# S and dP as rows: streaming transposed K and V past a 32-column weight in a decode attention backward

## The chip, the cores and the metric

One core of one Trainium2 chip runs the whole kernel. The metric is the device time of one execution in microseconds. The profile is one profiled execution of the same program; times inside it count from the start of its span.

## The reference

One token (B = Sq = 1, D = 640) goes through attention over a cache of 4096 keys in 32 heads of 128, and through a dense layer with Mish (F = 1728); a sigmoid gate mixes both. Computed are the output and the gradients of x, both caches, all weights, the bias and the gate. In bf16, K and V are 32 MB each, and dK and dV are as large.

```
q = (x @ wq) per head;  S = q . K * 128**-0.5;  p = softmax(S);  o = p @ V;  a = o @ wo
h = x @ w1 + b1;  b = mish(h) @ w2;  g = sigmoid(x . gate_w);  out = g*a + (1-g)*b
backward, per head, with do = (g*dy) @ wo.T:
  dP = do . V;  D = sum(p*dP);  dS = p*(dP - D)
  dV = p (outer) do;  dK = dS (outer) q*scale;  dq = dS @ K * scale
  dwo = o (outer) g*dy;  dwq = x (outer) dq;  dx, dw1, db1, dw2, dgate_w
```

## The kernel before

A head's K and V lie in SBUF as 128 partitions with 32 rows of 128 each (`Kn`, `Vn`; `KBUFS` = 4 and `VBUFS` = 3 buffers). The order of the work is written out by hand: a loop over heads, in groups of four (G = 4, NG = 8), and an epilogue for the last head. Each engine runs its instructions in that order, and nearly all transfers are issued by SP (SyncE) in that order too.

For each head:

- `k_tr` and `v_tr` (by `tr_block`, L511) transpose K and V. Pairs of bf16 are taken as one f32 word, four 128x128 words go through TensorE into one of two `tr` banks, and ScalarE copies them (L517) to `KT` or `VT`, which share one buffer. A head's K is four such blocks.
- `scores` and `dP` (by `cols_mm`, L519) make S and dP as 128x32 columns: 32 matmuls each, with a 128x128 piece of the transposed tile as the weights and a window of `qz` or `doz` (q or do, zero-padded) as the 32 columns that stream. `scores` also takes the row maximum on VectorE.
- `softmax` (L548) takes the maximum over partitions by a transpose, `exps` the exponentials on ScalarE, `dP` the products with dP on VectorE (`pj`), `zd_mm` the two sums over partitions, `probs` (L571) makes p and dS on VectorE.
- `dv_out` and `dk_out` write a head's dV and dK as two VectorE products each (L583) into `o_sb` (four buffers) and store it (L593).
- `dq_o` (L605) multiplies K with dS and V with p: 16 matmuls of 128x512 whose weights are 4 columns wide and go to column groups 0, 32, 64 and 96 of one PSUM bank. `od_cp` copies the bank, `dqo_mm` transposes the copy in the next head, `dqo_red` adds it up.

In the loop over h, V of head h is transposed at the head's start, and K of head h+1 after `dP(h)`. A head ends with `load_k(h + 4)` and `load_v(h + 3)`. Steps of the group (`g_*` for the next group's q and do, `f_*` for the last group's weight gradients) and of the dense layer (`mlp_some` with a budget of VectorE time, `dw2_some`) are placed by the head's number hh in its group. wq comes in three pieces of 2, 4 and 2 groups (`WQP`), in buffers of their own size; the gradient of each is written in place and stored from there.

A transfer waits for the one that used its semaphore before it; transfers from SP and ACT share eight such semaphores in turn.

Of the kernel before, what the change touches and what calls it, by code (L numbers as in the profile page):

```python
# [7 lines left out]
ACT = mybir.ActivationFunctionType  # L8
# [8 lines left out]
def kernel(  # L17
# [25 lines left out]
    P = 128  # L43
# [19 lines left out]
    JH = J // 2  # L63
    W = 32

# [24 lines left out]
    const = ctx.enter_context(tc.tile_pool(name="const", bufs=1))  # L90
    KBUFS, VBUFS = 4, 3
    kv_in = ctx.enter_context(tc.tile_pool(name="kv_in", bufs=KBUFS))
# [23 lines left out]

    WQP = [(0, 2), (2, 6), (6, NG)]
    assert NG == 8
# [110 lines left out]
    def pair_mm(col):  # L229
        ps = grp([P, 2, G], F32, "pair_ps")  # L230
        for par in range(2):
            nc.tensor.matmul(ps[:, par, :], lhsT=unzip[:, par, :], rhs=col[:], start=True, stop=True)
        return ps

    def pair_cp(z, ps):
        for par in range(2):
            nc.vector.tensor_tensor(z[:, :, J - 2 + par * J:J + par * J],  # L237
                                    ps[:, par, :].unsqueeze(2).to_broadcast([P, G, 2]),
                                    half[:].unsqueeze(1).to_broadcast([P, G, 2]), ALU.mult)
# [7 lines left out]
    def g_qpair_cp(g):  # L247
        pair_cp(qz, groups[g].pop("pair"))

# [3 lines left out]
    def g_dopair(g):  # L253
        pair_cp(doz, pair_mm(groups[g].pop("col")))

# [252 lines left out]

    S_ps, DP_ps, OD_ps = {}, {}, {}
    KT, VT, dgms, es, zds, p4s, ds4s = {}, {}, {}, {}, {}, {}, {}  # L510
# [7 lines left out]

    def cols_mm(out, T, z):  # L519
        Tb = T[:].rearrange("p c r -> p (c r)").bitcast(BF16).rearrange("p (c r a) -> p c r a", r=P, a=2)  # L520
        for c in range(J // 2):
            for par in range(2):
                a = J - 2 - 2 * c + par * J
                nc.tensor.matmul(out, lhsT=Tb[:, c, :, par], rhs=z[:, a:a + J],  # L524
                                 start=(c == 0 and par == 0), stop=(c == J // 2 - 1 and par == 1))

    def k_tr(h, c):
        if h < H:
            if c == 0:
                KT[h] = kvT.tile([P, J // 2, P], F32, name="KT", tag="T")  # L530
            tr_block(kts[h], KT[h], c)

# [4 lines left out]

    def scores(h):
        if h >= H:
            return  # L540
        S_ps[h] = s_ps.tile([P, J], F32, name="S", tag="S")
        cols_mm(S_ps[h][:], KT.pop(h), qz[:, h % G, :])
        m32 = small.tile([P, 1], F32, name="m32", tag="m32")
        nc.vector.reduce_max(m32[:], S_ps[h][:], axis=AX.X)
        dgms[h] = small.tile([P, 1], F32, name="m_s", tag="m_s")
        nc.vector.tensor_scalar(dgms[h][:], m32[:], scale, None, ALU.mult)
# [8 lines left out]
    def exps(h, negM):  # L555
        es[h] = small.tile([P, J], BF16, name="e_bf", tag="e_bf")
        zds[h] = small.tile([P, 2], F32, name="zd", tag="zd")
        nc.scalar.activation(es[h][:], S_ps.pop(h)[:], ACT.Exp, bias=negM[:], scale=scale, accum_out=zds[h][:, 0:1])

    def dP(h):  # L560
        DP_ps[h] = s_ps.tile([P, J], F32, name="DP", tag="DP")
        cols_mm(DP_ps[h][:], VT.pop(h), doz[:, h % G, :])
        pj = small.tile([P, J], F32, name="pj", tag="pj")
        nc.vector.scalar_tensor_tensor(pj[:], in0=DP_ps[h][:], scalar=1.0, in1=es[h][:],  # L564
                                       op0=ALU.mult, op1=ALU.mult, accum_out=zds[h][:, 1:2])
# [4 lines left out]
    def probs(h, mx):  # L570
        rz = small.tile([P, 1], F32, name="rz", tag="rz")  # L571
        nc.vector.reciprocal(rz[:], mx[:, P:P + 1])
        negD = small.tile([P, 1], F32, name="negD", tag="negD")
        nc.vector.tensor_scalar(negD[:], mx[:, P + 1:P + 2], rz[:], -1.0, ALU.mult, ALU.mult)
        p4s[h] = p4b[h % 3][:, 0:J * 4].rearrange("p (j t) -> p j t", t=4)
        nc.vector.tensor_scalar(p4s[h], es.pop(h)[:].unsqueeze(2).to_broadcast([P, J, 4]), rz[:], None, ALU.mult)
        ds4s[h] = ds4b[h % 3][:, 0:J * 4].rearrange("p (j t) -> p j t", t=4)
        nc.vector.scalar_tensor_tensor(ds4s[h], in0=DP_ps.pop(h)[:].unsqueeze(2).to_broadcast([P, J, 4]),
                                       scalar=negD[:], in1=p4s[h], op0=ALU.add, op1=ALU.mult)
        zds.pop(h)  # L580
# [35 lines left out]
    def od_cp(h):  # L616
        od_sb[h] = small.tile([P, 4, Dh], F32, name="row_sb", tag="row_sb", bufs=1)
        nc.scalar.copy(od_sb[h][:].rearrange("p j d -> p (j d)"), od4[:])  # L618
# [85 lines left out]
    for hh in range(G):  # L704
        g_do(0, hh)
    scores(0)
    g_dodiag(0)
    g_dobc(0)
    g_docol(0)
    g_dopair(0)  # L710
    g_qs(0)

    for h in range(H - 1):
        g, hh = h // G, h % G
        nx, pv = g + 1 < NG, g > 0
        v_tr(h, 0)
        if hh == 0 and pv:
            g_docol(g)
        if hh == 3 and nx:
            g_qcol(g + 1)  # L720
        if h > 0:
            dqo_mm(h - 1)
        v_tr(h, 1)
        mx, negM = softmax(h)
        if h > 0:
            dqo_red(h - 1)
        if hh == 0 and pv:
            g_dopair(g)
        if h > 0:
            dk_out(h - 1)  # L730
        v_tr(h, 2)
        v_tr(h, 3)
        exps(h, negM)
        dP(h)
        k_tr(h + 1, 0)
        k_tr(h + 1, 1)
        zd_mm(h, mx)
# [94 lines left out]
    l_dqbf(0, 3)  # L832
    v_tr(h, 2)
    v_tr(h, 3)
    exps(h, negM)
    dP(h)
    zd_mm(h, mx)
    f_bc(g, 0, 3)
# [83 lines left out]
```

## Time and profile before

| | |
|---|---|
| runs | 406.1, 406.25, 406.46 us; median 406.25 |
| profiled execution, span | 403.4 us, 10458 instructions (the page has no other time for it) |
| busy: PE, PEld, DVE, ACT | 306.3, 242.3, 312.1, 224.0 us |
| HBM read and written | 82.03 and 82.03 MB, 407 GB/s over the span |
| DMA packets | 27380, 164.72 MB |
| chain that ended last | DMA 60%, PE 15%, DVE 14%, ACT 4%, issue 3% |

PE is TensorE's matmuls and PEld its weight loads; DVE is VectorE, ACT ScalarE. A row of a group shows line, engine and operation, out<-in, count | busy us, mean ns of one | idle time just before them and what ended it. A row of waits is: us in total, times, longest. A row of stretches is: length, then the busy us (and count) of PE, PEld, DVE, ACT and POOL, the granted TensorE clock, the DMA share and GB/s. The 40 slices of the page are 10.1 us each.

### The profile page before, as it was taken

What the parts mean: (1) busy time and instruction counts of PE and PEld (TensorE: products, weight loads), DVE (VectorE), ACT (ScalarE), POOL (GpSimd) and SP (SyncE); (2) the same over time, 40 slices, a digit from 0 to 9 for tenths busy, and PEclk for the clock granted to TensorE, in tenths of its full rate; (3) what the DMA queues carried; (4) which work ended last, traced back from release to release, by engine and by line L of the source; (5) the groups of instructions that cost most, each with busy time, mean ns of one, the idle gap of its engine ahead of it and who ended that gap; (6) DMA issues with size and microseconds to landing.
All of it is one profiled execution on the core that took longest, in us unless ns stands there. A gap on an engine that the chain in (4) does not pass through costs nothing.

```text
span 403.4 us, 10458 instructions
## 1 busy us (share of the span) xinstructions
PE 306.3 (76%) x4278; PEld 242.3 (60%) x4285; DVE 312.1 (77%) x875; ACT 224.0 (56%) x447; POOL 9.9 (2%) x25
## 2 busy tenths in 40 slices
PE   2689999859888996869787788778798794889500
PEld 1477677647677875656675566656686474677300
DVE  3636877958988797998998888669999984996730
ACT  2256566645555564655577574877676363475600
POOL 3000001000000000000000011000000000000000
PEclk9999999998989899998999997989989898699855
DMA  8999999999999999999999999999999999999892
GB/s 296 425 415 423 424 423 412 416 423 423 418 427 425 422 415 426 424 424 425 425 423 424 425 421 425 416 427 424 424 423 425 423 423 425 420 409 417 365 399 86
DMA packets 27380, 164.72 MB, mean 408 GB/s; under 512 B 2884, under 2 KB 3013, under 8 KB 10950
## 3 DMA queue, kind: packets, MB, share of 16 engines
q1 hardware_dynamic: 27026, 164.05, 97.9%
q8 instruction: 33, 0.54, 0.5%
q14 instruction: 13, 0.11, 0.1%
q0 software_dynamic: 256, 0.01, 0.0%
q10 hardware_dynamic: 52, 0.01, 0.0%
HBM read 82.03 MB, written 82.03 MB: 407 GB/s over the span
## 4 chain that ended last, share of the span: by engine, by line
DMA 60%; PE 15%; DVE 14%; ACT 4%; issue 3%; DVEq 0%; SPq 0%; ACTq 0%
DMA out_dram<-o_sb 38%; DMA Vn<-in_A_v_cache_dram 15%; DVE o_sb L583 8%; PE tr L516 6%; DMA wo_g<-in_A_wo_dram 5%; DMA wq_p<-in_A_wq_dram 2%; DVE junk L259 2%; PE od L611 2%; ACT VT L517 2%; PE dqo_ps L624 1%; ACT KT L517 1%; PE q_ps L212 1%; PE S L524 1%; PE h_ps L409 1%; DVE wq_p L379 1%
## 5 line engine op out<-in xcount | busy, mean ns | idle before, releaser
L517 ACT COPY KT<-tr 128x512 f32<-128x512 f32 x128 | 69.2, 588 | 54.7 <-PE tr L516 54.7
L516 PE MATMUL tr<-ident_f,Vn 128*128 128x128 f32 x512 | 83.3, 297 | 18.6 <-DMA Vn<-in_A_v_cache_dram 12.2
L517 ACT COPY VT<-tr 128x512 f32<-128x512 f32 x128 | 72.2, 585 | 38.2 <-PE tr L516 37.1
L583 DVE TENSOR_TENSOR o_sb<-qs_row,ds 128x2048 bf16<-128x2048 bf16 x64 | 75.4, 1220 | 18.9 <-DMA out_dram<-o_sb 18.7
L516 PEld LDWEIGHTS tr<-ident_f,Vn 128*128 128x128 f32 x512 | 62.7, 152 | 34.1 <-ACT VT L517 12.2
L516 PE MATMUL tr<-ident_f,Kn 128*128 128x128 f32 x512 | 75.1, 293 | 8.2 <-DMA Kn<-in_A_k_cache_dram 5.7
L583 DVE TENSOR_TENSOR o_sb<-do_row,p 128x2048 bf16<-128x2048 bf16 x64 | 75.3, 1218 | 0.0
L516 PEld LDWEIGHTS tr<-ident_f,Kn 128*128 128x128 f32 x512 | 59.9, 151 | 11.2 <-DVE ident_f L169 5.7
L618 ACT COPY row_sb<-od 128x512 f32<-128x512 f32 x32 | 18.8, 586 | 39.5 <-PE od L611 39.5
L524 PE MATMUL DP<-doz,VT 128*128 128x32 bf16 x1024 | 36.2, 178 | 2.8
L524 PEld LDWEIGHTS <-KT 128*128 128x128 bf16 x1024 | 33.4, 98 | 6.5 <-ACT KT L517 3.3
L524 PE MATMUL S<-qz,KT 128*128 128x32 bf16 x1024 | 35.6, 179 | 1.9 <-DVE qz L237 0.2
L524 PEld LDWEIGHTS <-VT 128*128 128x128 bf16 x1024 | 32.9, 97 | 6.4 <-ACT VT L517 5.7
L611 PE MATMUL od<-Kn,ds 128*4 128x512 bf16 x256 | 36.1, 407 | 0.0
L611 PE MATMUL od<-Vn,p 128*4 128x512 bf16 x256 | 36.1, 407 | 0.0
L552 DVE TENSOR_REDUCE negM<-mx 128x1 f32<-128x128 f32 x32 | 9.3, 289 | 23.9 <-PE mx L550 22.0
L259 DVE SCALAR_TENSOR_TENSOR junk<-wo_g,da_bc 128x640 bf16<-128x640 bf16 x32 | 26.3, 821 | 0.4
L568 PE MATMUL mx<-zd,ones_f 128*128 128x2 f32 x64 | 11.1, 243 | 18.9 <-DVE pj L564 18.8
L387 ACT ACTIVATE wo_g<-da_bc,o 128x640 bf16<-128x640 bf16 x32 | 24.6, 822 | 0.0
L329 DVE SCALAR_TENSOR_TENSOR junk<-wq_p,dq_bc 128x512 bf16<-128x512 bf16 x35 | 24.1, 687 | 0.5
L624 PE MATMUL dqo_ps<-ident_f,row_sb 128*128 128x128 f32 x128 | 21.7, 295 | 3.1 <-ACT dh_bc L493 1.1
L568 PEld LDWEIGHTS mx<-zd,ones_f 128*128 128x128 f32 x64 | 9.9, 196 | 22.3 <-DVE pj L564 22.0
(169 smaller groups left out, 326.1 us busy)
## 6 DMA issues: line engine op xcount, KB each, us to landing
out_dram<-o_sb SPq DMA_DIRECT2D x64, 1024.0 KB, 18.6
Kn<-in_A_k_cache_dram SPq DMA_DIRECT2D x32, 1024.0 KB, 19.2
Vn<-in_A_v_cache_dram SPq DMA_DIRECT2D x32, 1024.0 KB, 19.3
wo_g<-in_A_wo_dram SPq DMA_DIRECT2D x8, 640.0 KB, 19.7
out_dram<-wo_g SPq DMA_DIRECT2D x8, 640.0 KB, 19.2
wq_p<-in_A_wq_dram SPq DMA_DIRECT2D x2, 1280.0 KB, 8.4
wq_p<-in_A_wq_dram SPq DMA_DIRECT2D x1, 2560.0 KB
out_dram<-wq_p SPq DMA_DIRECT2D x2, 1280.0 KB
```

The costliest lines, as they stand in the source:

```text
L259: nc.vector.scalar_tensor_tensor(junk[:], in0=wos[g][:, hh, :], scalar=1.0, in1=da_bc[:], op0=ALU.mult, op1=ALU.mult, accum_out=gp["do_col ...
L329: nc.vector.scalar_tensor_tensor(junk[:, cs], in0=wqs[g][:, c, cs], scalar=1.0, in1=gp["dq_bc"][:, cs], op0=ALU.mult, op1=ALU.mult, accum_ ...
L387: nc.scalar.activation(wos[g][:, hh, :], da_bc[:], ACT.Copy, scale=groups[g]["o4"][:, hh:hh + 1])
L516: nc.tensor.transpose(tp[:, t, :], words[:, t * P:(t + 1) * P], ident_f[:])
L517: nc.scalar.copy(dst[:, c * (TB // 2):(c + 1) * (TB // 2), :], tp[:])
L524: nc.tensor.matmul(out, lhsT=Tb[:, c, :, par], rhs=z[:, a:a + J], start=(c == 0 and par == 0), stop=(c == J // 2 - 1 and par == 1))
L552: nc.vector.tensor_reduce(negM[:], mx[:, 0:P], axis=AX.X, op=ALU.max, negate=True)
L568: nc.tensor.matmul(mx[:, P:P + 2], lhsT=ones_f[:], rhs=zds[h][:], start=True, stop=True)
L583: nc.vector.tensor_tensor(dst[:, a:b, :].rearrange("p j (k t) -> p j k t", t=4), row.rearrange("p (k t) -> p k t", t=4).unsqueeze(1).to_br ...
L611: nc.tensor.matmul(od4[32 * c:32 * c + 4, :], lhsT=c4[:, 4 * jb:4 * jb + 16].rearrange("p (j t) -> p t j", t=4)[:, 0, :], rhs=N[:, jb:jb + ...
L618: nc.scalar.copy(od_sb[h][:].rearrange("p j d -> p (j d)"), od4[:])
L624: nc.tensor.transpose(od_sb[h][:, j * (P - 1):j * (P - 1) + P], t[:, j, :], ident_f[:])
```

## The change

S and dP become rows. q and do each are put into a weight of 128x32 per parity of the bf16 pair (`qz` and `doz`, zeros elsewhere), so that one such matmul streams 512 columns of `KT` (four words c, 4+c, 8+c, 12+c of the 16) and gives S in some of its 32 output rows. Four column groups c and two parities are eight matmuls for S, and eight more for dP accumulate into other rows of the same PSUM bank `rw`. `rows_cp` copies the bank on ScalarE, `rows_tr` transposes it back in four pieces to `sd`, whose strided columns are S and dP. The maximum of S moves behind it (`maxes`), and the product with dP stands alone (`pjs`).

V of head h+1 is transposed in head h, after K of h+1, and the first head's V in the prologue. V gets a fourth buffer and `load_v(h + 4)`. wq comes in four pieces of two groups in two buffers. Group steps change places: do of the next group is made ready earlier. The last 64 rows of dw2 leave in four transfers from ACT's queue.

```
-    KBUFS, VBUFS = 4, 3
+    KBUFS, VBUFS = 4, 4
-    WQP = [(0, 2), (2, 6), (6, NG)]
+    WQP = [(g, g + 2) for g in range(0, NG, 2)]
-        wqp[k] = wts.tile([P, RC, (z - a) * GD], BF16, name="wq_p", tag=f"wq_{z - a}", bufs=1)
+        wqp[k] = wts.tile([P, RC, (z - a) * GD], BF16, name="wq_p", tag="wq_p", bufs=2)
     load_k(3)
+    load_v(3)
-    qz = const.tile([P, G, 3 * J - 2], BF16, name="qz")
-    doz = const.tile([P, G, 3 * J - 2], BF16, name="doz")
+    qz = const.tile([P, G, 2, 2, 16], BF16, name="qz")
+    doz = const.tile([P, G, 2, 2, 16], BF16, name="doz")
-    def pair_cp(z, ps):
+    def pair_cp(z, ps, at):
-            nc.vector.tensor_tensor(z[:, :, J - 2 + par * J:J + par * J],
+            nc.vector.tensor_tensor(z[:, :, par, :, at],
...
-    def cols_mm(out, T, z):
-        Tb = T[:].rearrange("p c r -> p (c r)").bitcast(BF16).rearrange("p (c r a) -> p c r a", r=P, a=2)
-        for c in range(J // 2):
-            for par in range(2):
-                a = J - 2 - 2 * c + par * J
-                nc.tensor.matmul(out, lhsT=Tb[:, c, :, par], rhs=z[:, a:a + J],
-                                 start=(c == 0 and par == 0), stop=(c == J // 2 - 1 and par == 1))
+    rw = s_ps.tile([P, 4 * P], F32, name="rw", tag="rw")
+    def rows_mm(T, z, first):
+        Tb = T[:].rearrange("p k r -> p (k r)").bitcast(BF16).rearrange("p (t c r a) -> p c a t r", t=4, c=4, a=2)
+        for par in range(2):
+            for c in range(4):
+                nc.tensor.matmul(rw[32 * c:32 * (c + 1), :], lhsT=z[:, par, :, :].rearrange("p m u -> p (m u)"), rhs=Tb[:, c, par, :, :],
+                                 start=first and par == 0, stop=not first and par == 1)
-    def scores(h):
...
+    def k_rows(h):
+        rows_mm(KT.pop(h), qz[:, h % G], True)
+    def v_rows(h):
+        rows_mm(VT.pop(h), doz[:, h % G], False)
+    def rows_cp(h):
+        rw_sb[h] = small.tile([P, 4, P], F32, name="row_sb", tag="row_sb", bufs=2)
+        nc.scalar.copy(rw_sb[h][:].rearrange("p t r -> p (t r)"), rw[:])
+    def rows_tr(h):
+        t = rw_sb.pop(h)
+        x = s_ps.tile([P, 4, P], F32, name="sd", tag="sd")
+        for j in range(4):
+            nc.tensor.transpose(x[:, j, :], t[:, j, :], ident_f[:])
+        v = x[:].rearrange("p t r -> p (t r)").rearrange("p (j u) -> p j u", u=16)
+        sd[h] = (v[:, :, 0], v[:, :, 1])
+    def maxes(h):
+        m32 = small.tile([P, 1], F32, name="m32", tag="m32")
+        nc.vector.tensor_reduce(m32[:], sd[h][0], axis=AX.X, op=ALU.max)
...
```

The loop's body after the change, without the group's steps:

```
        k_tr(h + 1, 0)
        dqo_mm(h - 1)
        k_tr(h + 1, 1)
        mx, negM = softmax(h)
        dqo_red(h - 1)
        dk_out(h - 1)
        k_tr(h + 1, 2)
        k_tr(h + 1, 3)
        exps(h, negM)
        k_rows(h + 1)
        pjs(h)
        v_tr(h + 1, 0)
        v_tr(h + 1, 1)
        zd_mm(h, mx)
        probs(h, mx)
        v_tr(h + 1, 2)
        v_tr(h + 1, 3)
        dv_out(h)
        v_rows(h + 1)
        dq_o(h)
        rows_cp(h + 1)
        rows_tr(h + 1)
        od_cp(h)
        maxes(h + 1)
        load_k(h + KBUFS)
        load_v(h + VBUFS)
```

And of the rest:

```
         if h == H - 4:
...
-            nc.sync.dma_start(out_8[FM:F, :], w2_sb[0:FT, FR, :])
+            for a, b in ((0, 2), (2, 5), (5, 9), (9, FT)):
+                nc.scalar.dma_start(out_8[FM + a:FM + b, :], w2_sb[a:b, FR, :])
...
-            if g in (0, 4):
-                load_wqp(g // 4 + 1)
+            if g % 2 == 0 and g + 4 <= NG:
+                load_wqp(g // 2 + 1)
```

In the epilogue the last head's `v_tr` and `dP` are gone; they lie in the loop.

More of the change, by code (lines that the diff above doesn't have):

```diff
@@ L63 @@
     JH = J // 2
-    W = 32
     Kv = A_k_cache.rearrange("b h (p j) d -> (b h) p j d", p=P)
@@ L115 @@
     wqp = {}
-    WQP = [(0, 2), (2, 6), (6, NG)]
-    assert NG == 8
+    WQP = [(g, g + 2) for g in range(0, NG, 2)]
+    assert NG % 2 == 0
     def load_wqp(k):
         a, z = WQP[k]
-        wqp[k] = wts.tile([P, RC, (z - a) * GD], BF16, name="wq_p", tag=f"wq_{z - a}", bufs=1)
+        wqp[k] = wts.tile([P, RC, (z - a) * GD], BF16, name="wq_p", tag="wq_p", bufs=2)
         for g in range(a, z):
@@ L247, in g_qpair_cp @@
     def g_qpair_cp(g):
-        pair_cp(qz, groups[g].pop("pair"))
+        pair_cp(qz, groups[g].pop("pair"), 0)
     def g_docol(g):
@@ L253, in g_dopair, with g_dopair_cp @@
     def g_dopair(g):
-        pair_cp(doz, pair_mm(groups[g].pop("col")))
+        groups[g]["pair"] = pair_mm(groups[g].pop("col"))
+    def g_dopair_cp(g):
+        pair_cp(doz, groups[g].pop("pair"), 1)
     def g_do(g, hh):
@@ L507, in m_dw2 @@
         nc.scalar.activation(w2_sb[0:n, fc, :], db_bc[0:n, :], ACT.Copy, scale=act_f[0:n, fc:fc + 1])
-    S_ps, DP_ps, OD_ps = {}, {}, {}
     KT, VT, dgms, es, zds, p4s, ds4s = {}, {}, {}, {}, {}, {}, {}
@@ L517, in tr_block @@
         nc.scalar.copy(dst[:, c * (TB // 2):(c + 1) * (TB // 2), :], tp[:])
-    def cols_mm(out, T, z):
-        Tb = T[:].rearrange("p c r -> p (c r)").bitcast(BF16).rearrange("p (c r a) -> p c r a", r=P, a=2)
-        for c in range(J // 2):
-            for par in range(2):
-                a = J - 2 - 2 * c + par * J
-                nc.tensor.matmul(out, lhsT=Tb[:, c, :, par], rhs=z[:, a:a + J],
-                                 start=(c == 0 and par == 0), stop=(c == J // 2 - 1 and par == 1))
+    rw = s_ps.tile([P, 4 * P], F32, name="rw", tag="rw")
+    rw_sb, sd = {}, {}
+    def rows_mm(T, z, first):
[4 more added lines that the diff above has]
+                                 start=first and par == 0, stop=not first and par == 1)
     def k_tr(h, c):
[L528 to L531, printed above, removed]
+        if c == 0:
+            KT[h] = kvT.tile([P, J // 2, P], F32, name="KT", tag="T")
+        tr_block(kts[h], KT[h], c)
     def v_tr(h, c):
@@ L536, in v_tr @@
         tr_block(vts[h], VT[h], c)
-    def scores(h):
[L539 to L542, printed above, removed]
+    def k_rows(h):
[13 more added lines that the diff above has]
+    def maxes(h):
         m32 = small.tile([P, 1], F32, name="m32", tag="m32")
-        nc.vector.reduce_max(m32[:], S_ps[h][:], axis=AX.X)
+        nc.vector.tensor_reduce(m32[:], sd[h][0], axis=AX.X, op=ALU.max)
         dgms[h] = small.tile([P, 1], F32, name="m_s", tag="m_s")
@@ L557, in exps, with pjs @@
         zds[h] = small.tile([P, 2], F32, name="zd", tag="zd")
[L558 to L562, printed above, removed]
+        nc.scalar.activation(es[h][:], sd[h][0], ACT.Exp, bias=negM[:], scale=scale, accum_out=zds[h][:, 0:1])
+    def pjs(h):
         pj = small.tile([P, J], F32, name="pj", tag="pj")
-        nc.vector.scalar_tensor_tensor(pj[:], in0=DP_ps[h][:], scalar=1.0, in1=es[h][:],
+        nc.vector.scalar_tensor_tensor(pj[:], in0=sd[h][1], scalar=1.0, in1=es[h][:],
                                        op0=ALU.mult, op1=ALU.mult, accum_out=zds[h][:, 1:2])
@@ L577, in probs @@
         ds4s[h] = ds4b[h % 3][:, 0:J * 4].rearrange("p (j t) -> p j t", t=4)
-        nc.vector.scalar_tensor_tensor(ds4s[h], in0=DP_ps.pop(h)[:].unsqueeze(2).to_broadcast([P, J, 4]),
+        nc.vector.scalar_tensor_tensor(ds4s[h], in0=sd.pop(h)[1].unsqueeze(2).to_broadcast([P, J, 4]),
                                        scalar=negD[:], in1=p4s[h], op0=ALU.add, op1=ALU.mult)
@@ L616, in od_cp @@
     def od_cp(h):
-        od_sb[h] = small.tile([P, 4, Dh], F32, name="row_sb", tag="row_sb", bufs=1)
+        od_sb[h] = small.tile([P, 4, Dh], F32, name="row_sb", tag="row_sb", bufs=2)
         nc.scalar.copy(od_sb[h][:].rearrange("p j d -> p (j d)"), od4[:])
@@ L705 @@
         g_do(0, hh)
-    scores(0)
+    k_rows(0)
     g_dodiag(0)
@@ L710 @@
     g_dopair(0)
+    g_dopair_cp(0)
+    for c in range(4):
+        v_tr(0, c)
+    v_rows(0)
+    rows_cp(0)
+    rows_tr(0)
+    maxes(0)
     g_qs(0)
@@ L715 @@
         nx, pv = g + 1 < NG, g > 0
-        v_tr(h, 0)
-        if hh == 0 and pv:
-            g_docol(g)
+        k_tr(h + 1, 0)
+        if h > 0:
+            dqo_mm(h - 1)
+        k_tr(h + 1, 1)
         if hh == 3 and nx:
             g_qcol(g + 1)
-        if h > 0:
-            dqo_mm(h - 1)
-        v_tr(h, 1)
         mx, negM = softmax(h)
@@ L726 @@
             dqo_red(h - 1)
-        if hh == 0 and pv:
-            g_dopair(g)
         if h > 0:
             dk_out(h - 1)
-        v_tr(h, 2)
-        v_tr(h, 3)
-        exps(h, negM)
-        dP(h)
-        k_tr(h + 1, 0)
-        k_tr(h + 1, 1)
+        k_tr(h + 1, 2)
+        k_tr(h + 1, 3)
+        if hh == 3 and nx:
+            g_qpair(g + 1)
+            g_qpair_cp(g + 1)
+            g_docol(g + 1)
+        exps(h, negM)
+        k_rows(h + 1)
+        pjs(h)
+        v_tr(h + 1, 0)
+        if hh == 3 and nx:
+            g_dopair(g + 1)
+            g_dopair_cp(g + 1)
+        v_tr(h + 1, 1)
         zd_mm(h, mx)
@@ L742 @@
             f_dx(g - 1, 3)
+        if hh == 1 and nx:
+            g_do(g + 1, 0)
         if hh == 2 and nx:
-            g_do(g + 1, 0)
-        if hh == 3 and nx:
-            g_qpair(g + 1)
             g_do(g + 1, 3)
         probs(h, mx)
-        if hh == 3 and nx:
-            g_qpair_cp(g + 1)
         if hh == 0 and pv:
@@ L753 @@
             f_o4c(g - 1)
-        k_tr(h + 1, 2)
-        k_tr(h + 1, 3)
+        v_tr(h + 1, 2)
+        v_tr(h + 1, 3)
         if hh == 0 and pv:
             f_bc(g - 1)
-        if hh == 3 and nx:
+        if hh == 2 and nx:
             g_dodiag(g + 1)
         dv_out(h)
-        scores(h + 1)
-        if hh == 3 and nx:
+        v_rows(h + 1)
+        if hh == 2 and nx:
             g_dobc(g + 1)
         dq_o(h)
+        rows_cp(h + 1)
+        rows_tr(h + 1)
         od_cp(h)
+        maxes(h + 1)
         load_k(h + KBUFS)
@@ L799 @@
                 f_dwo_st(g - 1)
-            budget = 2.7
-        if hh == 2:
             if nx:
@@ L804 @@
                 g_do(g + 1, 2)
+            budget = 0.9
+        if hh == 2:
+            if nx:
                 g_q(g + 1)
-            budget = 0.9
+            budget = 2.7
         if hh == 3:
-            if g in (0, 4):
-                load_wqp(g // 4 + 1)
+            if g % 2 == 0 and g + 4 <= NG:
+                load_wqp(g // 2 + 1)
             if g + 2 < NG:
@@ L823 @@
     nc.vector.tensor_tensor(gg[:], g_all[:], omg_all[:], ALU.mult)
-    v_tr(h, 0)
+    mx, negM = softmax(h)
     dqo_mm(h - 1)
-    v_tr(h, 1)
-    mx, negM = softmax(h)
+    exps(h, negM)
+    pjs(h)
+    zd_mm(h, mx)
     dqo_red(h - 1)
@@ L832 @@
     l_dqbf(0, 3)
[L833 to L837, printed above, removed]
     f_bc(g, 0, 3)
```

## The prediction

> **What bounds the kernel now.** I read the page first: busy time, the slices, the DMA queues.
>
> ```profile
> PE 306.3 (76%) x4278; PEld 242.3 (60%) x4285; DVE 312.1 (77%) x875; ACT 224.0 (56%) x447; POOL 9.9 (2%) x25
> ...
> DMA  8999999999999999999999999999999999999892
> GB/s 296 425 415 423 424 423 412 416 423 423 418 427 425 422 415 426 424 424 425 425 423 424 425 421 425 416 427 424 424 423 425 423 423 425 420 409 417 365 399 86
> ...
> q8 instruction: 33, 0.54, 0.5%
> ```
>
> No engine is busy above 77%, while the sixteen DMA engines are full from the first slice to the last but two, near 425 GB/s. So bytes set the time: 164.72 MB at 425 GB/s are 388 us, of 403.4. The rest must lie at the ends, so next the busy time by stretches:
>
> ```profile
> 350.00:372.00 22.00, 19.50 (x301) 15.96 (x298) 18.29 (x52) 15.85 (x33) 0.00 (x0) 1.00 1.01 411
> 372.00:378.00 6.00, 4.24 (x66) 2.87 (x65) 3.44 (x9) 2.59 (x7) 0.00 (x0) 1.00 0.81 333
> ...
> 394.00:396.00 2.00, 0.00 (x0) 0.00 (x0) 0.00 (x0) 0.00 (x0) 0.00 (x0) 0.50 0.53 218
> 396.00:398.00 2.00, 0.00 (x0) 0.00 (x0) 0.00 (x0) 0.00 (x0) 0.00 (x0) 0.50 0.07 28
> 398.00:400.00 2.00, 0.00 (x0) 0.00 (x0) 0.00 (x0) 0.00 (x0) 0.00 (x0) 0.50 0.07 29
> 400.00:402.00 2.00, 0.00 (x0) 0.00 (x0) 0.00 (x0) 0.00 (x0) 0.00 (x0) 0.50 0.06 25
> ```
>
> The last two columns are DMA share and GB/s. From 396 to 402 the share is 0.07, one engine of sixteen: fifteen are done at 395.0 to 395.7, one at 402.1. The trace's records of single packets show how that one fell behind. A `wo` transfer has packets of 5120 bytes that nothing else of that time has, so its end can be timed per engine. First and last engine end 9.7 and 10.9; then 103.1 and 105.5; 148.7 and 153.2; 212.2 and 219.0; 279.0 and 288.4; 327.5 and 338.8; 367.6 and 379.3. The late engine loses 11.7 us while the leaders keep the pace of their bytes. Its packets run back to back: it never lacks work, its own load sets the end, and only its load or a hole in its queue can move the time. At 372 to 378 the leaders starve instead, waiting for stores whose last sixteenth is with the late engine; so the gap at the end is 6.4 to 7.1, not 11.7.
>
> Then the waits, for the room that compute has:
>
> ```profile
> DVE o_sb L583 <- DMA out_dram<-o_sb: 18.7, 10, 5.9
> ...
> PE tr L516 <- DMA Vn<-in_A_v_cache_dram: 12.2, 12, 1.8
> ```
>
> Those 30.9 us over some 26 heads are 1.2 us a head. From head 5 to head 27 `dq_o` starts 11.44 us apart (78.8 to 330.4), so compute alone would need about 10.2.
>
> **The change, part by part.** First PE:
>
> ```profile
> L611 PE MATMUL od<-Kn,ds 128*4 128x512 bf16 x256 | 36.1, 407 | 0.0
> L524 PE MATMUL S<-qz,KT 128*128 128x32 bf16 x1024 | 35.6, 179 | 1.9 <-DVE qz L237 0.2
> L524 PEld LDWEIGHTS <-KT 128*128 128x128 bf16 x1024 | 33.4, 98 | 6.5 <-ACT KT L517 3.3
> L624 PE MATMUL dqo_ps<-ident_f,row_sb 128*128 128x128 f32 x128 | 21.7, 295 | 3.1 <-ACT dh_bc L493 1.1
> ```
>
> Gone are 2048 matmuls with a weight load each; new are 32 x 16 = 512 row matmuls and 32 x 4 = 128 transposes, each with its load. PE's 4278 + 4285 = 8563 instructions become 8563 - 4096 + 1280 = 5747.
>
> On PE's path this saves nothing. The old S needed KT block by block: 24 of its 32 matmuls ran under ACT's fourth copy, and `od` began 0.36 us after that copy (37.75 to 38.11). A row matmul of group c reads words c, 4+c, 8+c, 12+c, one from each copy, so all eight wait for the fourth. Their price is not in the trace; the nearest row is `od`, also 512 columns into four column groups, where fours start 0.21 us apart in the timeline (29.56, 29.77, 29.99, 30.20): eight are 2 x 0.21 + 0.17 = 0.6. One after another at `od`'s 0.38 they would be 3.0. I take 0.6, as the groups and width are `od`'s; the stride of two elements in the streamed side is what could make it 1.0. So +0.24 per use, twice a head; `rows_tr` adds 0.5 to 0.66 (L624's four). Together about 1.1 us a head: 10.2 + 1.1 = 11.3, just under 11.44, and so hidden by DMA. ACT gets a copy of 128x512 a head, 32 x 0.586 = 19 us, to 243 of 403; it stands before `od_cp`, and that one's readers come a head later. Behind the waiting row matmuls on PE stand `v_tr` and `zd_mm`; DVE's `probs` waits for those, and the 1.1 has it all in. `maxes` now waits for `rows_tr`, under `dv_out` (2 x 1.22) on DVE; without that cover it is 0.66 more.
>
> PE's instructions are themselves DMA traffic. Queue q8's 33 packets are 16,384 bytes each; 8563 / 33 = 259 instructions a packet, so 5747 make 22. The first comes at 27.5 us, the last at 372.4, 10 to 11 apart, each 0.9 to 1.1 us long (0.5% of sixteen engines' span is 32 us of one engine). The late engine's delays come in lumps of about 0.6 us, near many of these packets, and 0.6 is what 16,384 bytes cost at its pace (8192 in 0.306). Before the first packet the ends lie within 1.1 us. So I charge the lag to the fetches: 11.7 / 33 = 0.355 each, 11 fewer: -3.9. The bounds: spread evenly, 11 x 0.96 / 16 = -0.7; all on the late engine, 11 x 0.96, capped by the others' end at 395.7, -6.4. I take the measured slope.
>
> The Trainium skill, "Runtime: NRT & Kernel Launch", Instruction fetch mechanics, has the same blocks (16 KiB, 256 instructions) and says that crossing one is mostly hidden; by it this term is 0 and the sum 406.65. It speaks of the sequencer's wait, and no run here shows that wait apart.
>
> Smaller parts. `wq` in four pieces: the middle 2.62 MB move in rows of 2048 bytes, which follow each other every 80 ns, instead of 4096 every 155; per engine 80 x 80 for 40 x 155, +0.2 on the load and +0.2 on the store, on the late engine too: +0.4. The 64 rows of `out_8` in four pieces: 0 to 8 rows an engine for 4, at some 0.05 us a row, -0.2 to +0.2: 0. They move from SP to ACT (some 0.3 us each, in one head, where ACT has room), and take four of the eight semaphores that transfers share; SP's store of dK of head 27 may so wait for them, which the seven transfers still in flight cover (17 us); without them it would cost some 7. V and K of head h+4 are issued together and V's fourth buffer replaces the head by which it is now read earlier: 0. `g_do`, `g_dodiag` and the budgets change places between heads: 0, the same work under the same cover.
>
> The start is where a hole could open. Today the first store is issued at 30.7 us, and the loads ahead of it run dry at 36.6 to 38.6 (the ends of `w2`'s 6400-byte packets). The loop's first head now comes after four more transposed blocks and the row chain: two more pairs of blocks of K and V (some 1.4 each), the row copy and transposes (1.3), and the waits: I get 36.5. V of head 3 adds 1.05 MB, 2.5 us, so the loads last to 39 or 41. Some 2 us of room: 0, with a bound of +3.
>
> Sum against the profiled execution: 403.4 - 3.9 + 0.4 = 399.9. The median of the runs, 406.25, lies 2.85 above that span, taken as unchanged: 402.75, say 402.7.
>
> **The rivals.** *The lag is the engine's own.* For: other engines lose time too (at 327 ten are 4 to 6 us behind the first five), more than 33 fetches explain evenly; five packets of this size I could place (at 149.1, 192.9, 235.9, 260.8, 326.7) delayed another engine. Against: no lag before the first fetch, no lump after the last, only 0.5 us from 339 to 379, when PE was slow. Then the change is +0.4 less at most 0.7: 406.0 to 406.7, no difference that a measurement of this kernel can tell (0.2%, 0.8 us). "DMA: Bandwidth & Descriptors" of the Trainium skill, Latency and other measured facts, says that engines 7 and 15 are usually slower, which would be this case. Chance 0.13.
>
> *PE's head becomes longer than DMA's.* The place is `k_rows` and `v_rows`, which stop PE until the fourth copy. Room is 1.2 us a head; from there each further 0.1 us costs 29 x 0.1. Row matmuls of 0.8 instead of 0.6 give 1.5 added, +0.3 a head: +9, less part of the 3.5: 411 to 415. Half speed (1.0) gives about 425. For: the room is nearly spent; a hole at the start would come on top. Against: `od` runs this very shape in fours, DVE (9.75 us a head) is left alone. Chance 0.33, from just over 407 up.
>
> *All fetches sit on the late engine:* 406.25 - 6.4 + 0.4 = 400.2. Against: the five just placed. Chance 0.04.
>
> **How the numbers follow.** The forecast has 0.50, from 401 to 405: its slope is uncertain by a third. It and the last rival are faster, 0.54; the engine's own lag is the same, 0.13; the longer head is slower, 0.33. The likeliest case gives 402.7. Below 400.2 I leave 0.03; above 411 half of the slower case: 0.16.
>
> **What would show it.** Right: q8 near 22 packets, one engine alone at the end for some 3 us instead of 6.4, DMA still near 425 in the middle, row matmuls in fours 0.21 apart. Wrong: 22 packets and the same lone engine for 6 us (the lag is its own); or slices in the middle below 415 GB/s and PE's waits on ACT's copies above the DMA waits (a longer head); or a dip near 36 to 42 us (the start).

## The result, and the profile after

The changed kernel takes 421.51 us (median; 418.22 to 423.30), the kernel before 406.36 on the same chip: 1.0369 times, 95% interval 1.0324 to 1.0415, or some 15 us slower. Forecast were 402.7 us and a range that ended at 411. Of the rivals it was the longer head, and worse than its 411 to 415. Of all runs below, one of ten of e7_early_start, three of six of e8_late_do (its profile too) and one of twelve of e11_fill_copy_wait lie over 1.5% above the fastest of their kernel and are left out of the figures.

The page after, in the parts that were shown of before (busy time; DMA slices of 10.5 us; the fetch queue), and the chain that ended last:

```profile
span 421.5 us, 7650 instructions
PE 307.5 (73%) x2870; PEld 215.2 (51%) x2877; DVE 316.1 (75%) x875; ACT 241.5 (57%) x479; POOL 10.7 (3%) x25
...
DMA  7999997999999999999989999999989999979997
GB/s 276 429 417 421 389 428 307 361 411 415 426 416 421 410 376 427 388 401 417 424 356 362 424 413 426 417 417 424 372 326 333 416 397 417 384 292 422 405 363 286
...
q8 instruction: 22, 0.36, 0.3%
...
PE 43%; DVE 34%; ACT 15%; issue 3%; DMA 2%; DVEq 0%; ACTq 0%; SPq 0%
```

The chain was DMA 60% before and is DMA 2% now. Sixteen slices lie under 400 GB/s, spread over the whole span; before there were four, the first and three at the end. PE and VectorE are busy for hardly longer than before (+1.2 and +4.0 us), and ScalarE for 17.5 us more, the added copies; so what costs time is not more work but more waiting. The waits of after (us in total, times, longest) say for what:

```profile
DVE m L561 <- PE sd L555: 29.0, 24, 6.9
...
PE rw L528 <- ACT VT L519: 20.8, 32, 0.7
...
PE rw L528 <- ACT KT L519: 16.9, 25, 0.7
...
ACT VT L519 <- PE pair_ps L232: 16.6, 7, 3.2
...
PE rw L528 <- DVE qz L237: 10.5, 7, 1.9
...
DVE doz L237 <- PE pair_ps L232: 10.1, 8, 2.0
...
PE tr L518 <- DMA Kn<-in_A_k_cache_dram: 5.9, 1, 5.9
```

The two rows of before that gave the forecast its room, VectorE waiting for stores (18.7) and PE for V (12.2), are gone. PE's one wait for K is the first load. In their place stand waits of engine for engine. The groups of the row matmuls and of the maximum (line, engine, operation, count | busy, mean ns of one | idle time before them and what ended it):

```profile
L528 PE MATMUL rw<-KT,qz 128*32 128x512 bf16 x256 | 22.3, 425 | 27.4 <-ACT KT L519 16.9
L528 PE MATMUL rw<-VT,doz 128*32 128x512 bf16 x256 | 22.8, 434 | 20.8 <-ACT VT L519 20.8
...
L561 DVE TENSOR_REDUCE m<-sd 128x1 f32<-128x32 f32 x32 | 6.1, 190 | 29.7 <-PE sd L555 29.0
```

Two kinds of wait stand out: the row matmuls of nearly every head wait for the fourth copy (20.8 + 16.9 = 37.7 us), and seven or eight times, once a group, `qz`, `doz` and the copies behind them wait for the columns of the next group's q and do (10.5, 10.1 and 16.6 us).

The timeline of one such head, hh = 3, in order (start, us, engine, what; in brackets the idle time before it):

```profile
207.18 0.25 PE L223 MATMUL col_ps<-ones_bf,q_row 1*128 1x1 bf16 x4
...
207.85 0.16 DVE L226 CAST col<-col_ps 128x4 bf16<-128x4 f32 x1
...
208.20 2.35 DVE L598 TENSOR_TENSOR o_sb<-qs_row,ds 128x2048 bf16<-128x2048 bf16 x2
208.42 0.19 PE L232 MATMUL pair_ps<-col,unzip 128*128 128x4 bf16 x2
...
210.47 0.26 DVE L237 TENSOR_TENSOR qz<-pair_ps,half 128x8 bf16<-128x8 f32 x2
...
210.71 0.88 PE L528 MATMUL rw<-KT,qz 128*32 128x512 bf16 x8 [1.92 <-DVE qz L237]
...
212.72 0.27 DVE L237 TENSOR_TENSOR doz<-pair_ps,half 128x8 bf16<-128x8 f32 x2 [1.84 <-PE pair_ps L232]
212.73 0.58 ACT L519 COPY VT<-tr 128x512 f32<-128x512 f32 x1 [3.22 <-PE pair_ps L232]
```

The pairs are ready on PE at 208.6, but their copy into `qz` stands behind `dk_out` on VectorE (208.20 to 210.55), and PE's `k_rows` stands still for it. Then do's columns run PE, VectorE, PE, VectorE once more, with ScalarE's V copies behind them. Before, `qz` was wanted at the end of this head and `doz` only in the next, and do's columns were made there too, at the start of hh = 0.

**Where 18.1 us of span went**, by the starts of `dq_o` in the two profiled executions: head 0 at 29.6 before and 37.4 after, +7.8; from there to head 5, 49.3 and 55.5, +6.2; heads 5 to 28, 269.5 and 280.9, +11.4; to the last head +1.0; and from there to the end 28.1 and 19.9, -8.3, since DMA has less left to drain. From head 5 to 27 the pitch is 12.30 us (270.5 / 22) for 11.44, and in after nothing in that stretch waits for DMA: 12.3 is what compute needs, on the average of these heads.

### The profile page after: what moved, and what is told of

It is laid out like the page before. It is cut to its first block, busy times and chain, and to the rows that moved or that the text cites. A ratio compares the mean times of both kernels' runs of the same rounds, so it can differ in the third digit from the quotient of the medians.

```text
span 421.5 us, 7650 instructions
## 1 busy us (share of the span) xinstructions
PE 307.5 (73%) x2870; PEld 215.2 (51%) x2877; DVE 316.1 (75%) x875; ACT 241.5 (57%) x479; POOL 10.7 (3%) x25
## 4 chain that ended last, share of the span: by engine, by line
PE 43%; DVE 34%; ACT 15%; issue 3%; DMA 2%; DVEq 0%; ACTq 0%; SPq 0%
PE tr L518 15%; DVE o_sb L598 15%; ACT VT L519 8%; PE rw L528 8%; PE od L626 6%; PE sd L555 4%; DVE junk L262 3%; DVE junk L332 3%; DVE junk L479 3%; ACT KT L519 3%; DVE wq_p L382 2%; PE q_ps L212 2%; DMA wq_p<-in_A_wq_dram 2%; PE mx L583 1%; ACT wo_g L390 1%
## 5 line engine op out<-in xcount | busy, mean ns | idle before, releaser
L519 ACT COPY VT<-tr 128x512 f32<-128x512 f32 x128 | 69.9, 587 | 68.1 <-PE tr L518 51.3
L518 PE MATMUL tr<-ident_f,Kn 128*128 128x128 f32 x512 | 80.0, 292 | 20.7 <-ACT KT L519 13.8
L518 PE MATMUL tr<-ident_f,Vn 128*128 128x128 f32 x512 | 80.6, 306 | 1.3 <-ACT VT L519 1.0
L518 PEld LDWEIGHTS tr<-ident_f,Kn 128*128 128x128 f32 x512 | 61.1, 148 | 29.6 <-ACT KT L519 20.7
L518 PEld LDWEIGHTS tr<-ident_f,Vn 128*128 128x128 f32 x512 | 64.5, 160 | 18.1 <-issue 14.9
L528 PE MATMUL rw<-KT,qz 128*32 128x512 bf16 x256 | 22.3, 425 | 27.4 <-ACT KT L519 16.9
L528 PE MATMUL rw<-VT,doz 128*32 128x512 bf16 x256 | 22.8, 434 | 20.8 <-ACT VT L519 20.8
L626 PE MATMUL od<-Kn,ds 128*4 128x512 bf16 x256 | 37.4, 417 | 0.0
L561 DVE TENSOR_REDUCE m<-sd 128x1 f32<-128x32 f32 x32 | 6.1, 190 | 29.7 <-PE sd L555 29.0
L549 ACT COPY row_sb<-rw 128x512 f32<-128x512 f32 x32 | 18.8, 587 | 15.7 <-PE rw L528 15.7
L633 ACT COPY row_sb<-od 128x512 f32<-128x512 f32 x32 | 18.7, 586 | 12.5 <-PE od L626 12.5
L555 PEld LDWEIGHTS sd<-ident_f,row_sb 128*128 128x128 f32 x128 | 14.3, 148 | 17.8 <-ACT row_sb L549 17.0
L555 PE MATMUL sd<-ident_f,row_sb 128*128 128x128 f32 x128 | 22.2, 299 | 1.3 <-ACT row_sb L549 1.3
L528 PEld LDWEIGHTS <-qz 128*32 128x32 bf16 x256 | 6.6, 95 | 32.3 <-issue 21.2
## 6 DMA issues: line engine op xcount, KB each, us to landing
Kn<-in_A_k_cache_dram SPq DMA_DIRECT2D x32, 1024.0 KB, 10.5
Vn<-in_A_v_cache_dram SPq DMA_DIRECT2D x32, 1024.0 KB, 12.2
wo_g<-in_A_wo_dram SPq DMA_DIRECT2D x8, 640.0 KB, 11.6
```

What stands on the lines that cost most here:

```text
L518: nc.tensor.transpose(tp[:, t, :], words[:, t * P:(t + 1) * P], ident_f[:])
L519: nc.scalar.copy(dst[:, c * (TB // 2):(c + 1) * (TB // 2), :], tp[:])
L528: nc.tensor.matmul(rw[32 * c:32 * (c + 1), :], lhsT=z[:, par, :, :].rearrange("p m u -> p (m u)"), rhs=Tb[:, c, par, :, :], start=first an ...
L549: nc.scalar.copy(rw_sb[h][:].rearrange("p t r -> p (t r)"), rw[:])
L555: nc.tensor.transpose(x[:, j, :], t[:, j, :], ident_f[:])
L626: nc.tensor.matmul(od4[32 * c:32 * c + 4, :], lhsT=c4[:, 4 * jb:4 * jb + 16].rearrange("p (j t) -> p t j", t=4)[:, 0, :], rhs=N[:, jb:jb + ...
```

## Experiments

Medians of the kernel before were 405.5 to 406.0 in these batches, 0.4 to 0.9 below its median beside after, so runs of different batches are compared by their ratio to it. All are summed up here. Two of them leave something out, so their S and dP are not those of the task: e1_no_refresh keeps the first group's q and do, and e6_no_copy_wait streams a constant in place of K and V.

| run | what it is | us | ratio to before (95%) |
|---|---|---|---|
| after | the changed kernel | 421.5 | 1.0369 (1.0324 to 1.0415) |
| e1_no_refresh | no refresh of the columns | 409.7 | 1.0119 (1.0085 to 1.0154) |
| e2_early_columns | early columns | 408.5 | 1.0060 (1.0033 to 1.0087) |
| e3_columns_in_new_order | S, dP as columns, late steps | 413.2 | 1.0188 (1.0169 to 1.0207) |
| e3b_columns_early | S, dP as columns, early steps | 410.2 | 1.0112 (1.0082 to 1.0142) |
| e6_no_copy_wait | no copy wait | 407.4 | 1.0028 (1.0010 to 1.0045) |
| e12_fill_copy_wait_in_after | copy wait filled | 415.4 | 1.0226 (1.0194 to 1.0258) |
| e5_small_parts | small parts in before | 405.4 | 0.9995 (0.9984 to 1.0007) |
| e10_do_early_in_before | do early in before | 407.3 | 1.0030 (1.0015 to 1.0045) |
| e4_more_fetches | more fetches in before | 412.0 | 1.0148 (1.0122 to 1.0173) |
| e7_early_start | early columns, early start | 409.2 | 1.0067 (1.0036 to 1.0099) |
| e8_late_do | early columns of q, late do | 411.9 | 1.0126 (1.0095 to 1.0157) |
| e11_fill_copy_wait | the same, copy wait filled | 406.4 | 1.0019 (0.9995 to 1.0044) |
| e13_early_and_fill | early columns, copy wait filled | 408.1 | 1.0046 (1.0030 to 1.0063) |
| e14_wo_later | and wo asked for later | 405.1 | 0.9986 (0.9969 to 1.0003) |
| e15_early_start | and early start | 404.7 | 0.9974 (0.9960 to 0.9988) |
| e16_work_under_sd | and work under sd | 405.0 | 0.9976 (0.9964 to 0.9987) |

**The columns of q and do.** First without them, then with all of them, made earlier:

```
# no refresh: these six calls of the loop are dropped
-            g_qcol(g + 1)
-            g_qpair(g + 1)
-            g_qpair_cp(g + 1)
-            g_docol(g + 1)
-            g_dopair(g + 1)
-            g_dopair_cp(g + 1)
# early columns: all kept; g_q at the end of hh = 1, then
+ hh = 2:   k_tr(h+1,1); g_qcol; ...; k_tr(h+1,3); g_qpair; ...; k_rows(h+1); pjs; g_qpair_cp
+ hh = 3:   g_docol; k_tr(h+1,0); dqo_mm; k_tr(h+1,1); g_dopair; softmax; dqo_red; g_dopair_cp; dk_out
```

> After without the column steps of groups 1 to 7 in the loop (g_qcol, g_qpair, g_qpair_cp, g_docol, g_dopair, g_dopair_cp): the weights of the first group serve all heads, so S and dP of heads 4 to 31 are those of other q and do. All other work stays. Theory A (boundary): the columns of q and do for the next group are now made and used inside one head (hh = 3), which in after ends 13.7 us after the one before it where it took 10.8 before, seven times; without them 402 to 406, DMA near 425 GB/s again. Theory B (rows): what costs is paid in every head, the row matmuls that wait for the fourth copy (37.7 us of PE's waits) and the chain over rw, row_sb and sd; then only some 5 us are won: 414 to 418.

> After with the same column steps made earlier and nothing left out: g_q of the next group at the end of hh = 1, its columns in hh = 2 (written to qz behind k_rows, the last reader), the columns of do from the start of hh = 3 and written to doz ahead of dk_out. Theory A: like the run without the steps, 402 to 406, and PE's wait of k_rows for qz (10.5 us) and of the copies for pair_ps (16.6 us) gone. Theory B: 413 to 418. A third way: the steps now delay hh = 2 by as much as they delayed hh = 3: 418 to 422.

Both fell, to 409.7 and 408.5, between the two cases written above and nearer to the first. Of the 3.69% that the change costs, the early columns win 3.09%, some 12.5 us, though PE's wait for the fourth copies is as large as in after (40.4 us for 37.7):

```profile
PE rw L528 <- ACT VT L519: 20.8, 32, 0.7
PE rw L528 <- ACT KT L519: 19.6, 30, 0.7
```

The `dq_o` intervals that end in a head of hh = 3 (heads 7 to 27) average 13.4 us in after, 11.9 without the steps, 10.9 with early ones and 10.7 before. The boundary is a cause; but neither run came to before.

**Rows or columns.** After's order with the old `cols_mm`, once with the late steps and once with the early ones:

```
     def k_rows(h):
-        rows_mm(KT.pop(h), qz[:, h % G], True)
+        S_ps[h] = s_ps.tile([P, J], F32, name="S", tag="S")
+        cols_mm(S_ps[h][:], KT.pop(h), qz[:, h % G, :])     # v_rows alike, into DP
-        rows_cp(h + 1)
-        rows_tr(h + 1)
```

> After's order, V buffers and small parts, but S and dP made as columns as before (32 matmuls each into S and DP at the places of k_rows and v_rows, no rows_cp and rows_tr). Theory A: the boundary is in it whole, so it stays slow, 412 to 422. Theory B: the rows are what costs, so it is near before, 404 to 408. If both pay: between, 408 to 412.

> Columns (S and DP by 32 matmuls each, as in e3_columns_in_new_order) in after's order, with the column steps of q and do made early (as in e2_early_columns). With the two earlier runs this makes four corners: rows or columns, late or early steps. If the two costs add up (late steps 13, rows 8.3 with late steps): 400 to 402, below what DMA leaves; so near 405, the floor of before. If the rows cost nothing by themselves: 408.5 as with rows.

With late steps the rows cost 1.0369 against 1.0188, 7.3 us; with early steps 1.0060 against 1.0112, nothing, rather 2 us less. So no price of the rows in each head shows: they cost where the head is already stretched. These are net prices, since the kernels with columns also fetch 33 and 34 packets for the rows' 22, and what that difference is worth here was not measured. And the new order with columns and early steps is still 1.1% slower than before, so part of the cost is the order and not the rows. I had expected the fourth corner at 405; it missed that by 5 us, and its longest chain names `wo` (21%), which comes up again below.

**The wait for the fourth copy.** Once taken away (the row matmuls stream a constant), once filled with work, PE's transposes of the next tile's first block:

```
# no copy wait
-        Tb = T[:].rearrange("p k r -> p (k r)").bitcast(BF16).rearrange("p (t c r a) -> p c a t r", t=4, c=4, a=2)
+        Tb = ident_f[:].bitcast(BF16).rearrange("p (r a) -> p a r", a=2)
...                                          # the matmul streams it broadcast over t
# copy wait filled (tr_pe: the four transposes of tr_block; the copy stays where it was)
+        pend["v", h + 1, 0] = tr_pe(vts[h + 1], 0)
         k_rows(h + 1)
...
+        if h + 2 < H:
+            pend["k", h + 2, 0] = tr_pe(kts[h + 2], 0)
         v_rows(h + 1)
```

> After, but the row matmuls stream a constant (the identity, broadcast to 512 columns) instead of KT and VT: S and dP are then without meaning, the work and its order stay, and no row matmul waits for a copy. Prices the place that the rival named, the wait for the fourth copy (37.7 us of PE's waits in after). If that wait is on the path of every head: 421.5 less 0.6 x 2 x 29, some 35, capped by DMA: 405 to 410. If the boundary's columns hold the head anyway and PE has slack elsewhere: 414 to 420.

> After, correct as it is, with the same filling of the waits for the fourth copies and nothing else. In after PE waits 37.7 us for these copies; the transposes put there take 0.57 each, 62 of them, 35 us. If the wait is on the path in most heads: 421.5 - 10 to 14, 407 to 411. If the late columns of q and do alone hold the heads: 418 to 422.

407.4 and 415.4. Taking the wait away wins as much as the early columns (3.4%, 14 us), with the late columns left in; it frees the row matmuls from all four copies, and also starts the first `dq_o` 5.0 us earlier (32.4 for 37.4). Filling the wait, which delays what comes behind by the transposes' own time, wins 1.4%, 6 us, between the two cases written above. With the wait gone the chain lies on VectorE:

```profile
DVE 55%; PE 25%; DMA 11%; ACT 3%; issue 2%; SPq 1%; DVEq 0%; ACTq 0%
```

So 12.5 and 14 us do not add up to the 15 lost: either seems to bring most heads back to DMA's pace, and what is won below it does not count. That a repair wins this much tells that PE's wait lies on the path; whether the change brought it there is looked at below.

**The parts costed at nothing**, each alone in the kernel before. The small parts are V's fourth buffer, `wq` in four pieces and the four transfers of `out_8`; the other run has `g_do`, `g_dodiag`, `g_dobc` and the budgets at after's places, a head earlier:

```
-        if hh == 2 and nx:
+        if hh == 1 and nx:
             g_do(g + 1, 0)
...
-        if hh == 3 and nx:
+        if hh == 2 and nx:
             g_dodiag(g + 1)          # g_dobc alike; g_do 1, 2 to the end of hh = 1, g_do 3 to hh = 2
```

> Before with only the small parts of the change: V's fourth buffer, wq in four pieces of two groups, the last rows of dw2 in four transfers from ACT. The prediction's sum: +0.4, so 406.6 to 406.8, within what can be told from no change. Rival: the moved transfers hold SP up, as they do in after for 9.9 us in one head: +1 to +5 if the transfers in flight do not cover it.

> Before with one step of the change alone: g_do, g_dodiag, g_dobc and the budgets at the places that after gives them, a head earlier; columns, scores, dP and buffers as before. The prediction put 0 on this. If VectorE then waits for wo whenever DMA is full (landing 19.7 us after the issue in before, and asked for some 17 us after it): seven waits of 2 to 7 us, and 409 to 415. If the head has room for it: 405.5 to 406.5.

The small parts make no difference, 0.9995. Do made early costs 0.3%, 1.2 us (0.6 to 1.8), between the two cases written above. Its waits show why it is not more:

```profile
DVE junk L259 <- DMA wo_g<-in_A_wo_dram: 17.5, 6, 8.6
...
DVE o_sb L583 <- DMA out_dram<-o_sb: 3.1, 3, 1.6
PE tr L516 <- DMA Vn<-in_A_v_cache_dram: 2.8, 2, 1.8
```

VectorE now waits 17.5 us for `wo`, up to 8.6 at a time, but the waits for stores and V shrink from 18.7 and 12.2 to 3.1 and 2.8. DMA was the bound; the wait moved. In after the same `g_do` waits for nothing: DMA is no longer full there, and `wo` lands 11.6 us after its issue instead of 19.7.

**The fetches.** Instructions added to an idle engine, in the kernel before:

```
+        nc.gpsimd.tensor_copy(pg[:], dgms[h + 1][:])
+        for _ in range(80):
+            nc.gpsimd.engine_nop()
```

> Before with 80 empty GpSimd instructions in each of 31 heads, behind a small copy of that head's maximum that spreads them over the run: 2480 instructions on an engine that is else idle. If the instruction fetches make the late DMA engine late at the measured slope (0.355 us each), some 9.7 fetches more: before +3.4 us, and the lone engine at the end some 9 to 10 us behind instead of 6.4. If the lag is the engine's own: 0 to +0.6. If only TensorE's instructions are fetched in this way: q8 stays at 33 packets and the run tells nothing.

It took 6.0 us more (5.0 to 7.0). No wait for GpSimd came with it: the one in the trace, 2.3 us at the start, is in before too. The fetch queues of its page:

```profile
q8 instruction: 33, 0.54, 0.5%
q14 instruction: 33, 0.27, 0.2%
```

In before q8 is the same, and q14 is:

```profile
q14 instruction: 13, 0.11, 0.1%
```

GpSimd's packets come on q14, 20 more of 8192 bytes each, as many bytes as ten of PE's, so the third case written above does not apply. The late engine is done with the last `wo` at 403.7 instead of 397.2, fourteen of the others by 396.2 instead of 389.8. I had expected the lone engine alone to fall back by 3; it and the rest fell back by some 6.5 together. That the rest starve for its buffers would explain this, but is not shown. In its stretches (columns as before) the lone engine is at work from 402 on, where it was from 396:

```profile
400.00:402.00 2.00, 0.00 (x0) 0.00 (x0) 0.00 (x0) 0.00 (x0) 0.00 (x0) 0.50 0.87 357
402.00:404.00 2.00, 0.00 (x0) 0.00 (x0) 0.00 (x0) 0.00 (x0) 0.00 (x0) 0.50 0.07 31
404.00:406.00 2.00, 0.00 (x0) 0.00 (x0) 0.00 (x0) 0.00 (x0) 0.00 (x0) 0.50 0.07 29
```

The lag in mid-run grew, from 11.2 us at 327 to 13.7 at 330. An extra fetch of 8192 bytes cost the run 0.3 us, about as long as such a packet takes in the trace (0.31).

**Putting it together.** From the early columns on: an early start alone, do made late, and the fill on top of that:

```
# early start: V(0) transposed ahead of do's columns; head 0's softmax .. dv_out ahead of k_tr(1, 2)
# late do: g_do 0 in hh = 2, 1 to 3 at its end; diagonal, broadcast, columns, doz within hh = 3
```

> e2_early_columns with a shorter start: the first V's blocks ahead of the columns of do, and p and dV of head 0 before K of head 1 is transposed. If the 7.8 us by which dq_o of head 0 is late (37.4 for 29.6) are lost for good, because later heads are no faster than DMA: 4 to 5 us off e2_early_columns's 408.5, to 403.5 to 405, and the dip of 364 GB/s near 75 us gone. If DMA's backlog makes up for the start anyway: 408.

> e2_early_columns with do of the next group made as late as it can be (g_do in hh = 2, diagonal, broadcast, columns and doz all within hh = 3), so that VectorE no longer asks in hh = 1 for a wo that was issued at the end of the group before. If VectorE's wait for wo (8.3 us in e2_early_columns, none in before or after) is what keeps the repaired kernel above before: 408.5 - 4 to 6, so 402.5 to 405, with no wait of L262 on wo. If making do inside hh = 3 brings the boundary back: 410 to 415.

> e8_late_do with PE's waits for the fourth copies filled: the transposes of the next tile's first block (V after K, the next head's K after V) go ahead of the row matmuls, their copies stay behind. If heads are still longer than DMA's: 1 to 4 us off e8_late_do. If e8_late_do is back at DMA's pace: the same within 1 us, near 403.

The early start brought nothing (1.0067 for 1.0060) though the first `dq_o` moved from 35.1 to 32.4. Do made late cost 0.7% (three runs), and the wait for `wo` is gone, also in the profile of the run with the fill on top: the second case, the boundary came back. Filling the copy wait then won 1.1%, 4.3 us, a little more than the 1 to 4 expected. The last four runs put fill and early columns together and go on from there:

```
# wo later, on top of early columns and fill
-        if hh == 1 and nx:
-            g_do(g + 1, 0)           # was ahead of probs
...
+                g_do(g + 1, 0)       # at the end of hh = 1, ahead of g_do 1 and 2
# work under sd: f_dx(g - 1, 0), f_dx(g - 1, 4) or g_qs(g + 1) ahead of maxes
```

> e2_early_columns (early columns of q and do) with the filling of the waits for the fourth copies. If the two prices were both on the path and only DMA's floor stood below: 402.5 to 405 (402.7 would be the prediction's own sum, with 22 fetches; 406 a floor that the fetches do not move). If the early g_do waits for wo as in e2_early_columns (8.3 us): 405 to 408.

> e13_early_and_fill with the first g_do of the next group moved from the middle of head hh = 1 to its end, some 4 us later, where the wo it needs has had more time to land. If the wait for wo is what is left: 1 to 4 us below e13_early_and_fill and the wait of L262 on wo under 2 us. If not: the same.

> e14_wo_later with the shorter start of e7_early_start (the first V ahead of the columns of do, p and dV of head 0 ahead of the next K). If the late start is a loss of its own: 2 to 4 us below e14_wo_later. If DMA's backlog makes it up, as it seemed in e7_early_start: the same within 1 us.

> e15_early_start with one piece of VectorE's work of the head's end (a product of 0.7 for wq's gradient in hh = 0 and 1, qs_row in hh = 3) ahead of maxes, where VectorE waits some 0.9 us a head for rows_tr. If that wait is on the path: 1 to 3 us below e15_early_start. If DMA sets the pace by then: the same.

Fill and early columns alone stayed at 408.1, with VectorE's wait for `wo` (the early columns alone have 8.3):

```profile
DVE junk L262 <- DMA wo_g<-in_A_wo_dram: 9.0, 5, 4.8
```

Moving one `g_do` by some 4 us took that wait away and won 0.6%, 2.4 us. The early start then gave 404.7, 0.26% below before and the first to be faster with an interval that excludes 1; over the run without it the gain is 0.1%, too small to tell. Work under `sd` changed nothing: DMA sets the pace again, as its slices in the fastest run (e15_early_start) show,

```profile
GB/s 275 425 417 420 420 422 418 404 420 425 422 426 423 425 415 425 419 424 425 427 420 422 428 415 425 424 418 426 424 425 423 425 414 424 365 367 423 383 387 221
```

with 23 fetches instead of 33, and with the late engine back: at its last `wo` 396.4 against 393.0 for fourteen others. At the very end it is hardly alone, 401.3 against some 400.6, since the others have work for longer than in before (402.1 against 395.7).

## Why the prediction was wrong

**What held.** DMA bounds the kernel before; 22 fetch packets; the small parts near 0 (measured 0.9995, at most +0.3 us, so `wq`'s +0.4 was a little too much). The eight row matmuls cost what was taken: 0.63 to 0.64 in the trace at full clock, for 0.6; so the stride of two elements shows no price here. The rival of the longer head thus had the outcome right, but not its price: it wanted row matmuls of 0.8 or 1.0, and that 1.0 gives 425 there, near the measured time, is chance.

**The step that failed: "`g_do`, `g_dodiag` and the budgets change places between heads: 0, the same work under the same cover".** The work was the same, the time by which it is wanted was not. V a head ahead means that `doz` is needed inside hh = 3, and the row matmuls of K need `qz` in the middle of that head instead of at its end. The sentence does not name the steps that make them, four hops between PE and VectorE for each, though the change moves these too: do's from the start of the next head into hh = 3, and q's last two ahead of `exps`. So both are made and used within one head, with `dk_out` ahead of q's last hop and of do's second. Early columns are worth 12.5 us. The prediction asked who waits for the row matmuls but never who makes their weights. What the sentence does name, `g_do` a head earlier, is worth 1.2 us in before and, for its first `g_do` alone, 2.4 in the repaired kernel, by a `wo` that has not landed. Together that is 14.9 of the 15 us lost, in the order in which the repairs were made; between them stands the fill with 0.6, and it gave 6 when it came first, so the split depends on the order.

**The 1.1 us a head is not that step.** A use of K's rows takes PE (22.3 + 16.9) / 32 = 1.23 us with its wait for the copy; the old scores took (35.6 + 3.3) / 32 = 1.22 with the wait of their weight loads, the time of the copies filled with matmuls; for V it is 1.36 and 1.31. And rows cost nothing net against columns once the steps are early. That the run without the copy wait wins 14 us says that PE is on the path of a head, not that the change brought the wait's time. The sum was 11.3 and compute takes 12.3; of the 1.0 between, the late columns make (13.4 - 10.9) / 4 = 0.6. The other 0.4 is not settled. One candidate is the 10.2 itself: it takes off the waits of two engines as if they added up, and no run shows that they do. Another is the cover that the forecast gave `maxes`, `dv_out`: VectorE waits for `sd` 24 times, 29.0 us, so it does not hold; but work put there in the last run brought nothing, with DMA setting the pace again.

**The room was an average.** 1.2 us a head came from two waits spread evenly. But the intervals of before that end in hh = 0 to 3 average 12.7, 10.6, 12.5 and 10.7, and the change loaded the heads unevenly: 10.8, 11.3, 13.0, 13.4 in after. A head of 13.4 is not made good by one of 10.8 once DMA's queue has run empty; what DMA then stands still, as the slices show, is not got back. How much of the loss comes by this was not measured.

**The start** was taken at 0 with a bound of +3. The first store is issued at 38.6 (forecast 36.5; 30.7 before), and by head 5 compute is 14 us behind, with slices of 307 and 361 GB/s at 63 to 84 us. That the start is a loss of its own is not shown: repaired, it gave between nothing and 0.1%.

**The fetches.** -3.9 was not tested by the change, since the end was no longer set by the late engine: the last `wo` ends within some 0.2 us on all engines in after. The experiments bear the mechanism out, where DMA stays full. In the five profiles that move 421 to 423 GB/s from 84 to 330 us, the lag near 330 to 340 us is 11.2 and 10.6 us with 33 fetches (before; small parts), 7.9 and 9.2 with 23 (the last two repaired kernels), 13.7 with 33 and 20 of half the size. An engine that is late by itself, the first rival, would show some 11 in each. Which of the sixteen the late one is, the packets' records here do not say. In the profiles below 420 GB/s the lag is 6.7 us or less whatever the number of fetches (6.7 with 33, do early in before; 4.2 with 22, `wo` later); there DMA has gaps, in which the late engine presumably catches up. The Trainium skill, "Runtime: NRT & Kernel Launch", Instruction fetch mechanics, has the crossing of a block as mostly hidden; for the sequencer that may be so, but here the fetch's bytes pass through the DMA engines that the data need, and 20 more cost 6.0 us. How much ten fewer bring is still not measured by itself: the fastest run is 1.1 us below before, with a later end of compute (last `dq_o` at 381.3 for 375.2) against it. Why the rows cost 7.3 us with the late steps alone was not taken apart either; that their longer chain (copy, transposes, maximum) lies right behind the late `qz` is argued.

## What to carry to other kernels

When a step is moved earlier, list the operands that it now needs earlier, and follow each to its maker: here the matmuls moved ahead, their small weight columns were made right in front of them, and one hop behind a long product on VectorE became the wait. A repair that wins what was lost does not name the cause: taking PE's wait for the copies away won 14 us, though the kernel before had spent the same time there. Compare the sum with the limit head by head and not on the average, since a wait of a few heads empties the queue that the others would need.

## What the runs showed of the hardware

Empty instructions on an engine that was busy for 2% of the span are not free: 2480 of them are fetched in 20 packets of 8192 bytes through the same DMA engines, and a kernel bound by these got 6.0 us longer. In the five profiles whose DMA stayed full (421 to 423 GB/s), the lag of the latest DMA engine followed the number of fetches (7.9 to 13.7 us).
